# A new static order for an attention and two-MLP kernel: PSUM banks taken in turns, two-bank QK products, and small steps moved between engines

## The chip, the cores and the metric

The kernel runs as one program on one core of a Trainium2 chip. The metric is the device time of one execution in microseconds (us). Engines are named as the profile names them: PE (matrix multiply; PEld is its weight load), DVE (vector), ACT (scalar), POOL (GpSimd), and SP, whose queue issues nearly all DMAs. PSUM is the memory into which PE writes; the kernel holds it as one tile `pb` of eight banks of 512 words.

## The reference

```python
scores = scale * np.matmul(q, k.transpose(0, 1, 3, 2))        # 2 batches, 8 heads, 768 tokens, 64 dims
scores = np.where(keep, scores + bias, -1e9)                  # own 96 tokens back, and the first 8
a = np.exp(scores - max); a = a / (np.sum(a) + 1e-09)
x = np.matmul(a, v)                                           # laid out as (1536 tokens, 512)
h = x @ w_in                                                  # 512 -> 2048
P = a[0] + a[1]*h + a[2]*h**2 + a[3]*h**3
Q = 1.0 + np.abs(b[0])*np.abs(h) + np.abs(b[1])*h**2
x = (P / (Q + 1e-06)) @ w_out                                 # 2048 -> 512
h = x @ w_in2                                                 # 512 -> 1024
solu = h * softmax(h); ln = (solu - mean) / np.sqrt(var + 1e-06) * g_ln
out = ln @ w_out2                                             # 1024 -> 512
```

The weights come as 64-bit floats and are narrowed to 32 bits on the chip.

## The kernel before, in words

`record` writes down every piece of work as an operation (`op`) with an engine, an assumed duration, what it reads and writes, and a priority. `Plan.run` then goes through them as a list scheduler: at each step it takes the engine that can start earliest and, among the operations ready there within 0.15 us, the one with the smallest `due - lead`. The order in which it emits them is the static order of every engine, and the semaphores are put in for that order. Where two engines use the same PSUM bank, the emitted order also sets who goes first: the second one waits for the first, whether or not there is a data dependence. The planner before does not know of this; it lets two engines read a bank at the same time.

The work has these parts:

- Attention, in 48 units of one 128-token tile and two heads. `u_load` brings q, k (`qkt`) and v; `qk` (line 405) multiplies, DVE takes the bias and the minimum of both heads (`smax`, line 411), ACT exponentiates (418), DVE makes reciprocals (423, 424), POOL multiplies with them (`norm`, 429), PE transposes (446), ACT copies out (458), PE multiplies with v (`pv`, 453), and ACT and DVE split the result into a high and a low part (460 and line 82). q of each head is padded with zeros to 128 rows, so that one product per head runs over all 128 rows; both heads share one bank. The four units of a batch's first tile have 128 keys (n = 1), the others 256 (n = 2). The bias tables are made on DVE (369).
- The first MLP, over four blocks of 384 tokens: 64 steps of one block and one 128-wide slice f of the hidden dimension. Segments are (block 0, f 0 to 7), blocks 1, 2, 3 in full, and (block 0, f 8 to 15). A step has 12 products for h (574, 576, 580), the rational function on ACT and DVE (600 to 617; lines 602, 604, 607 read the bank of h on DVE and 600, 603, 606 on ACT), a low part on POOL (line 82, `g`), and three steps later 9 products into y (665, 666, 671). Attention of block 1 runs beside segment 0, of block 2 beside segment 1, of block 3 beside segment 2 (`UW`).
- 48 weight pieces of 128 x 512 (32 of the first MLP, 16 of the second), each loaded (485), scaled into a PSUM bank by ACT (509), its sign bits cleared in place by POOL (526), joined by two DVE operations (530, 518), cast to the high part by ACT (548) and subtracted to the low part by POOL (line 82, `w`).
- The second MLP, for twelve tiles: transposes of y (731), 24 products (750 to 752), softmax and normalisation on DVE and ACT (772 to 799), eight transposes (812), 24 products (834 to 836), copy and store (843, 845).

SP, like every engine, goes through its own list in the order emitted.

Of the kernel before, what the change touches and what calls it, by code (L numbers as in the profile page):

```python
# [30 lines left out]
UW = {1: (0, 7), 2: (8, 15), 3: (24, 15)}  # L31
# [3 lines left out]
M2 = (41, 22)  # L35

ZS = range(48)
# [3 lines left out]
WLEAD = 2.0  # L41


SLOW = (5.0, 1.2)
# [82 lines left out]
class Plan:  # L127
# [4 lines left out]
    SEM = 0.05  # L132
# [7 lines left out]
    def op(self, eng, lat, fn, r=(), w=(), new=(), occ=None, lock=False, lead=0.0, move=0.0, after=(), tag=""):  # L140
        o = Op()
        o.i, o.eng, o.lat, o.fn, o.lock, o.lead, o.move, o.tag = len(self.ops), eng, lat, fn, lock, lead, move, tag
# [44 lines left out]

    def settle(self, n):
# [13 lines left out]
    def run(self, emit=True):  # L202
        self.deadlines()
        self.pools = {p: [(0.0, s) for s in sl] for p, sl in self.slots.items()}
        for v in {v for o in self.ops for v in o.vals}:
            v.left, v.free = len(v.users), 0.0
# [6 lines left out]
        at = {e: 0.0 for e in ready}  # L213
# [3 lines left out]
        def add(o):  # L217
            o.t0 = max((d.end for d in o.deps), default=0.0) + self.SEM
            ready[o.eng].append(o)
# [5 lines left out]
        while left:  # L225
            best = None
            for e, l in ready.items():
                c = []
                for o in l:
                    t = max(o.t0, at[e])  # L230
                    ok = True
                    need = {}
                    for v in o.new:
# [3 lines left out]
                        need[v.pool] = need.get(v.pool, 0) + 1  # L237
                        fr = self.pools[v.pool]
                        if self.line[v.line][x][0] is not v or len(fr) < need[v.pool]:
                            ok = False  # L240
                            break
                        t = max(t, sorted(fr)[need[v.pool] - 1][0])
# [22 lines left out]
            at[e] = t + o.occ  # L265
            o.end = t + o.lat
            if o.lock:
                port = t + o.occ
            if e == "SP":
                dma = max(dma, at[e]) + o.move  # L270
                o.end = dma + o.lat
            for v in o.vals:
                v.left -= 1
# [26 lines left out]
def record(tc, es, const, qkv, w_in, w_out, w2_in, w2_out, coef, g_sb, nv, ident, out):  # L300
# [52 lines left out]
    def bias_keep():  # L353
# [11 lines left out]
        dve.tensor_scalar(out=kp, in0=kp, scalar1=-1.0, scalar2=-MASK, op0=ALU.add, op1=ALU.mult)  # L365
# [7 lines left out]
    op("DVE", 2.0, bias_keep, w=vt0)  # L373
    for p in range(4):
        op("DVE", 0.9, lambda p=p: bias_pair(p), r=vt0, w=[vbias[p]], lock=True)
# [4 lines left out]
    xs = {}  # L380
# [9 lines left out]
    def u_load(u):  # L390
        u.qk, u.v = Val("qk"), Val("v")
        w = 256 + u.w
        uop("SP", 2.0, lambda: sync.dma_start(out=qkt[u.qk.slot][:, 0:w], in_=qkv[u.t, u.p, :, 0:w]), occ=0.4,
# [796 lines left out]
```

## Time and profile before

| | us |
|---|---|
| median of 3 runs (568.31 to 568.39) | 568.36 |
| the profiled execution | 569.23 |
| its span, first to last instruction | 567.4 |
| busy: PE, DVE, ACT, POOL | 529.6, 429.2, 390.2, 223.9 |
| mean granted clock of PE, share of full speed | 0.989 |

The profiled execution lies 1.83 us above its own span and 0.87 us above the median. Matmuls overlap in the profile, so a busy PE is not PE at its peak. The span falls into six stages by what PE does: up to the first h product at 45.3 us (attention of block 0), segment 0 (to 97.6), segment 1 (to 192.2), segment 2 (to 287.4), segments 3 and 4 with their y products (to 417.4), and the second MLP, whose last 24 first products end at 538.1.

### The profile page before, as it was taken

How to read it: one execution, taken by the hardware profiler on the slowest of the kernel's cores; microseconds unless marked ns; L12 is line 12 of the kernel's file. 1: busy time of each engine (PE TensorE's matmuls, PEld its weight loads, DVE VectorE, ACT ScalarE, POOL GpSimd, SP SyncE). 2: the span in 40 equal slices, each digit the busy share in tenths (PEclk: the TensorE clock that was granted, in tenths of full speed). 3: DMA queues.
4: the chain of work that ended last, by engine and by line, in shares of the span. 5: the costliest groups of instructions: out<-in, count | busy, mean ns of one | idle time of the engine just before them, and what ended most of it. 6: DMA issues, size and time to landing. Idle time of an engine off the chain costs nothing.

```text
span 567.4 us, 8749 instructions
## 1 busy us (share of the span) xinstructions
PE 529.6 (93%) x2808; PEld 437.8 (77%) x2808; DVE 429.2 (76%) x1045; ACT 390.2 (69%) x903; POOL 223.9 (39%) x278
## 2 busy tenths in 40 slices
PE   4899998999989899999999989998999999999985
PEld 2567887878877688888887877877878888888865
DVE  6777888998999997677679999889866555555540
ACT  4788888898988888777788887877634444433331
POOL 3675456546677743332335563756400000000000
PEclk9999999999999999999999999999999999999989
DMA  7779255533444443110043230233001111000001
GB/s 247 244 259 324 89 167 161 165 102 94 130 160 152 134 133 114 36 58 26 2 149 130 75 115 34 76 111 104 25 21 39 40 54 37 22 35 20 18 20 43
DMA packets 28278, 56.24 MB, mean 99 GB/s; under 512 B 3520, under 2 KB 11968, under 8 KB 28224
## 3 DMA queue, kind: packets, MB, share of 16 engines
q1 hardware_dynamic: 28080, 55.59, 30.0%
q8 instruction: 24, 0.39, 0.3%
q14 instruction: 30, 0.25, 0.1%
q10 hardware_dynamic: 144, 0.00, 0.0%
HBM read 47.72 MB, written 7.86 MB: 98 GB/s over the span
## 4 chain that ended last, share of the span: by engine, by line
PE 51%; DVE 27%; ACT 15%; issue 4%; POOL 1%; DMA 1%; ACTq 0%; SPq 0%; POOLq 0%; DVEq 0%
PE pb L834 4%; PE pb L836 4%; PE pb L835 4%; PE pb L405 4%; PE pb L750 4%; PE pb L752 4%; PE pb L751 4%; DVE t L615 3%; DVE t L604 3%; DVE t L602 3%; PE pb L453 3%; PE pb L574 3%; PE pb L665 3%; PE pb L580 3%; DVE t L613 3%
## 5 line engine op out<-in xcount | busy, mean ns | idle before, releaser
L82 POOL TENSOR_TENSOR g<-t,g 128x384 fp32r<-128x384 f32 x64 | 69.4, 1084 | 79.9 <-ACT g L617 74.2
L574 PE MATMUL pb<-x,w 128*128 128x384 f32 x256 | 90.0, 352 | 5.4 <-DVE t L607 5.2
L576 PE MATMUL pb<-x,w 128*128 128x384 f32 x256 | 86.2, 337 | 0.0
L665 PE MATMUL pb<-w,g 128*128 128x512 f32 x192 | 78.3, 408 | 7.4 <-ACT g L617 6.3
L429 POOL TENSOR_SCALAR e<-e,st 128x256 f32<-128x256 f32 (+1 forms) x96 | 47.3, 505 | 75.0 <-DVE st L424 56.1
L666 PE MATMUL pb<-w,g 128*128 128x512 f32 x192 | 76.2, 397 | 0.0
L82 POOL TENSOR_TENSOR w<-wst,w 128x512 fp32r<-128x512 f32 x48 | 64.7, 1354 | 18.8 <-ACT w L548 16.2
L574 PEld LDWEIGHTS pb<-x,w 128*128 128x128 f32 x256 | 48.2, 188 | 14.0 <-DVE t L607 10.7
L580 PE MATMUL pb<-x,w 128*128 128x384 f32 x256 | 57.5, 346 | 0.0
L671 PE MATMUL pb<-w,g 128*128 128x512 f32 x192 | 57.2, 406 | 0.0
L405 PE MATMUL pb<-qk 128*128 128x256 f32 (+1 forms) x192 | 50.0, 392 | 6.7 <-DMA qk<-in_qkv 5.4
L602 DVE TENSOR_TENSOR t<-t,pb 128x384 f32<-128x384 f32 x64 | 35.1, 548 | 22.3 <-ACT t L603 20.8
L418 ACT ACTIVATE e<-e,st 128x256 f32<-128x256 f32 (+1 forms) x96 | 46.3, 486 | 5.3 <-DVE st L411 5.1
L665 PEld LDWEIGHTS pb<-w,g 128*128 128x128 f32 x192 | 36.3, 189 | 17.4 <-ACT g L617 9.3
L580 PEld LDWEIGHTS pb<-x,w 128*128 128x128 f32 x256 | 44.7, 188 | 6.2 <-issue 2.4
L576 PEld LDWEIGHTS pb<-x,w 128*128 128x128 f32 x256 | 48.3, 189 | 1.3
L405 PEld LDWEIGHTS pb<-qk 128*128 128x128 f32 x192 | 35.4, 208 | 12.9 <-DMA qk<-in_qkv 5.4
L606 ACT ACTIVATE pb<-pb 128x384 f32<-128x384 f32 x64 | 30.4, 476 | 20.9 <-DVE t L604 20.6
L600 ACT ACTIVATE t<-pb,coef 128x384 f32<-128x384 f32 x64 | 42.6, 666 | 2.6 <-PE pb L580 1.6
L617 ACT CAST g<-t 128x384 fp32r<-128x384 f32 x64 | 32.7, 512 | 16.9 <-DVE t L615 10.6
L607 DVE SCALAR_TENSOR_TENSOR t<-pb,coef,t 128x384 f32<-128x384 f32 x64 | 39.2, 612 | 6.8 <-ACT pb L606 6.1
L615 DVE SCALAR_TENSOR_TENSOR t<-t,coef,t 128x384 f32<-128x384 f32 x64 | 42.7, 667 | 0.7
(106 smaller groups left out, 1261.6 us busy)
## 6 DMA issues: line engine op xcount, KB each, us to landing
wst<-in_w_in SPq DMA_DIRECT2D x24, 512.0 KB, 4.3
wst<-in_w_out SPq DMA_DIRECT2D x24, 512.0 KB, 4.1
qk<-in_qkv SPq DMA_DIRECT2D x40, 256.0 KB, 3.2
v<-in_qkv SPq DMA_DIRECT2D x40, 128.0 KB, 2.5
y_d<-y SPq DMA_DIRECT2D x12, 256.0 KB, 2.7
y<-y_d SPq DMA_DIRECT2D x12, 256.0 KB, 2.6
out<-wst SPq DMA_DIRECT2D x11, 256.0 KB, 2.0
qk<-in_qkv SPq DMA_DIRECT2D x8, 192.0 KB, 3.3
```

What stands on the lines that cost most here:

```text
L82: eng.tensor_tensor(out=out, in0=a, in1=hi.bitcast(F32), op=ALU.subtract)
L405: pe.matmul(out=pb[:, u.s.slot, h * 256:h * 256 + w], lhsT=a[:, h * 128:(h + 1) * 128], rhs=a[:, 256:256 + w], start=True, stop=True)
L418: act.activation(out=e[:, h, 0:w], in_=e[:, h, 0:w], func=AF.Exp, scale=-1.0, bias=st[:, h:h + 1], accum_out=st[:, 2 + 2 * h:3 + 2 * h])
L429: pool.tensor_scalar(out=e[:, h, 0:w], in0=e[:, h, 0:w], scalar1=st[:, 6 + h:7 + h], scalar2=0.0, op0=ALU.mult, op1=ALU.add)
L574: pe.matmul(out=pb[:, g.h.slot, 0:n], lhsT=wt[wh.slot][:, cs[p]], rhs=xt[x[p][0].slot][:, 0:n], start=(p == 0), stop=False)
L576: pe.matmul(out=pb[:, g.h.slot, 0:n], lhsT=wt[wl.slot][:, cs[p]], rhs=xt[x[p][0].slot][:, 0:n], start=False, stop=False)
L580: pe.matmul(out=pb[:, g.h.slot, 0:n], lhsT=wt[wh.slot][:, cs[p]], rhs=xt[x[p][1].slot][:, 0:n], start=False, stop=(p == 3))
L602: op("DVE", 0.14 + 0.41 * k, lambda: dve.tensor_tensor(out=T(g.c), in0=T(g.c), in1=h(), op=ALU.mult), r=[g.h], w=[g.c], tag="ch")
L615: op("DVE", 0.15 + 0.41 * k, lambda: stt_(out=T(g.c), in0=T(g.c), scalar=coef[:, 0:1], in1=T(g.b), op0=ALU.add, op1=ALU.mult), r=[g.b], w= ...
L665: pe.matmul(out=pb[:, y[i].slot, :], lhsT=gt[g.gh.slot][:, c], rhs=wt[wh.slot], start=g.first, stop=False)
L666: pe.matmul(out=pb[:, y[i].slot, :], lhsT=gt[g.gh.slot][:, c], rhs=wt[wl.slot], start=False, stop=False)
L671: pe.matmul(out=pb[:, y[i].slot, :], lhsT=gt[g.gl.slot][:, c], rhs=wt[wh.slot], start=False, stop=g.last)
```

## The change

`Plan.run` keeps, for each value in a PSUM bank, the operation that used it last; a user on another engine may only start after that one's end. It also lets an operation that needs two buffers of one pool claim them against later-due ones, starts each engine's clock at a value of its own, and has other assumed durations, other gaps between the operations of POOL and DVE that it marks `lock` (these exclude each other in the plan), and a table of priorities (`LEADS`). In `record`: the attention units of blocks 0 and 3 take a bank for each head, and multiply 64 rows instead of 128; the bias tables go from DVE to ACT; `norm` goes from POOL to DVE for 19 of 48 units (`NDVE`); the sign bits of 22 of 48 weight pieces are handled by a second DVE operation instead of POOL's (`ZS`); 6 of 48 low parts go from POOL to DVE (`WDVE`); weight loads wait for the h products of the step before, and the second 16 weight pieces are spread over steps 8 to 22 (`WS`); the pieces of the second MLP are recorded over 17 steps instead of 22 (`M2`); and the weight pieces of segment 0 beyond the first four are recorded inside the steps.

```diff
+WS = (8, 14)
-UW = {1: (0, 7), 2: (8, 15), 3: (24, 15)}
+UW = {1: (0, 7), 2: (8, 15), 3: (25, 14)}
-M2 = (41, 22)
+M2 = (41, 17)
-ZS = range(48)
+ZS = (2, 4, 6, 8, 10, 12, 15, 17, 18, 20, 22, 24, 26, 28, 30, 32, 33, 34, 35, 36, 38, 40, 42, 44, 46, 47)
+START = ('hh',)
+BACK = (('y1', 'p'), ('y0', 'y2'))
+TWO = (3,)
+NDVE, WDVE = (3, 4, 5, 6, 7, 8, 9, 10, 11, 14, 15, 36, 38, 39, 40, 41, 42, 44, 46), (11, 20, 31, 42, 44, 45)
+BEGIN = {"PE": 2.0, "ACT": 5.0, "DVE": 3.4, "POOL": 1.0, "SP": 1.6, "X": 0.0}
+BANKS = ("h", "s", "p", "y0", "y1", "y2")
...
+                    for v in o.vals:
+                        if v.pool in BANKS and v.last is not None and v.last.eng != e:
+                            t = max(t, v.last.end + self.SEM)
...
-                        if o.lock:
-                            t = max(t, port)
-                        c.append((t, o))
+                        c.append((max(t, port - self.PORT) if o.lock else t, o, need))
+            for e, c in can.items():
+                c = [(t, o) for t, o, need in c if all(o.due - o.lead <= claims.get(p, 1e9) + CLAIM for p in need)]
...
+        dve.tensor_tensor(out=dz, in0=dz, in1=kp, op=ALU.add)
...
-            dve.scalar_tensor_tensor(out=bt[h], in0=dz, scalar=-8.0 * SLOPE[h], in1=kp, op0=ALU.mult, op1=ALU.add)
+            act.mul(bt[h], dz, -8.0 * SLOPE[h])
...
-                pe.matmul(out=pb[:, u.s.slot, h * 256:h * 256 + w], lhsT=a[:, h * 128:(h + 1) * 128],
-                          rhs=a[:, 256:256 + w], start=True, stop=True)
+                r = slice(h * 64, (h + 1) * 64) if two else slice(0, 128)
+                pe.matmul(out=score(h), lhsT=a[r, h * 128:(h + 1) * 128], rhs=a[r, 256:256 + w], start=True, stop=True)
...
-                pool.tensor_scalar(out=e[:, h, 0:w], in0=e[:, h, 0:w], scalar1=st[:, 6 + h:7 + h],
-                                   scalar2=0.0, op0=ALU.mult, op1=ALU.add)
+                (dve if ndve else pool).tensor_scalar(out=e[:, h, 0:w], in0=e[:, h, 0:w], scalar1=st[:, 6 + h:7 + h],
+                                                      scalar2=0.0, op0=ALU.mult, op1=ALU.add)
...
+        if nlo[0] - 1 in WDVE:
+            op("DVE", 0.68, lambda: minus(nc, dve, wt[lo.slot], src(), wt[hi.slot]), r=[st, hi], w=[lo], lock=True, lead=WLEAD, tag="wlo")
...
-            w_make(wseq[made[0]])
+            w_make(wseq[made[0]], [gs[-1].op] if gs else [])
...
-            make_to(2 * s + 4)
+            make_to(min(2 * s + 4, max(2 * SEGS[0][2], 2 * SEGS[0][2] + (s - WS[0]) * (32 - 2 * SEGS[0][2]) // WS[1])))
```

Three places of the order itself. POOL in block 0, before: its products with the reciprocals (line 429), sign bits of weight pieces (526) and low parts (82) alternate.

```order
L82 TENSOR_TENSOR w_95<-wst_157,w_94 128x512
L429 TENSOR_SCALAR e_214<-e_214,st_219 128x128 x2
L526 TENSOR_SCALAR wst_159<-wst_159 128x512
L82 TENSOR_TENSOR w_97<-wst_158,w_96 128x512
L429 TENSOR_SCALAR e_211<-e_211,st_220 128x256 x2
L429 TENSOR_SCALAR e_212<-e_212,st_221 128x256 x2
L526 TENSOR_SCALAR wst_156<-wst_156 128x512
L429 TENSOR_SCALAR e_213<-e_213,st_216 128x256 x2
```

The same place now (469 is the product with the reciprocals, 569 the sign bits, 97 the low part); from the fourth unit on, DVE does the products of block 0.

```order
L97 TENSOR_TENSOR w_93<-wst_156,w_92 128x512
L569 TENSOR_SCALAR wst_158<-wst_158 128x512
L97 TENSOR_TENSOR w_95<-wst_157,w_94 128x512
L97 TENSOR_TENSOR w_97<-wst_158,w_96 128x512
L97 TENSOR_TENSOR w_99<-wst_159,w_98 128x512
L469 TENSOR_SCALAR e_211<-e_211,st_216 128x256 x2
L469 TENSOR_SCALAR e_212<-e_212,st_217 128x256 x2
```

All but three units of block 0 left POOL, and the last two rows are already units of block 1. On DVE the same stretch now has, after the reciprocals (463, 464), the products (469), and for a piece without POOL's step two operations on the bank (556, 557) before the join (561).

```order
L556 SCALAR_TENSOR_TENSOR pb<-pb,wst_157 128x512
L557 SCALAR_TENSOR_TENSOR pb<-wst_157,pb 128x512
L451 ISA e_214,st_219<-pb,bt_202 128x128
L451 ISA st_219 128x1
L451 ISA e_214,st_219<-pb,bt_203 128x128
L451 ISA st_219 128x1
L561 SCALAR_TENSOR_TENSOR wst_157<-wst_157,pb 128x512
L463 TENSOR_SCALAR st_219<-st_219 128x2
L464 RECIPROCAL st_219<-st_219 128x2
L469 TENSOR_SCALAR e_214<-e_214,st_219 128x128 x2
```

Before, the piece had one operation on the bank (530) and no product stood there. The third place is PE's end. Before, after the output products of the tenth tile, the eight transposes of the eleventh tile (`wst_158`) are followed by four of the twelfth (`wst_156`), and only then come the products of the eleventh.

```order
L834 MATMUL pb<-w_123,lh_2892 128x512
L835 MATMUL pb<-w_122,lh_2892 128x512
L836 MATMUL pb<-w_123,ll_2894 128x512
L812 MATMUL pb<-ident,wst_158 128x128 x8
L812 MATMUL pb<-ident,wst_156 128x128 x4
L834 MATMUL pb<-w_109,lh_2891 128x512
L835 MATMUL pb<-w_111,lh_2891 128x512
```

Now the eleventh tile is `wst_156` and the twelfth `wst_158`; the last four transposes of the eleventh are followed at once by its products.

```order
L881 MATMUL pb<-w_123,lh_2892 128x512
L882 MATMUL pb<-w_122,lh_2892 128x512
L883 MATMUL pb<-w_123,ll_2894 128x512
L859 MATMUL pb<-ident,wst_156 128x128 x4
L881 MATMUL pb<-w_109,lh_2893 128x512
L882 MATMUL pb<-w_111,lh_2893 128x512
```

The twelfth tile's eight transposes moved behind those 24 products.

## Rows read from the trace of the kernel before

**Rows 1.** Windows, one stage each: stretch, length, busy us (instructions), PEclk, DMA.
```profile
0.00:45.30 45.30, 32.91 (x185) 22.46 (x185) 33.05 (x143) 31.32 (x98) 27.09 (x52) 0.96 0.75 246
45.30:97.60 52.30, 50.56 (x328) 41.58 (x326) 43.87 (x127) 45.91 (x122) 29.63 (x41) 1.00 0.56 184
97.60:192.20 94.60, 89.34 (x490) 73.83 (x488) 88.72 (x204) 82.64 (x196) 59.83 (x70) 0.98 0.43 138
192.20:287.40 95.20, 94.58 (x534) 79.58 (x535) 73.37 (x193) 74.88 (x180) 36.58 (x46) 1.00 0.20 62
287.40:417.40 130.00, 121.14 (x582) 103.09 (x582) 115.22 (x202) 100.78 (x200) 70.80 (x70) 1.00 0.26 89
417.40:538.10 120.70, 120.59 (x587) 100.04 (x586) 67.53 (x163) 48.02 (x99) 0.00 (x0) 1.00 0.10 33
538.10:567.40 29.30, 20.49 (x113) 17.27 (x111) 7.47 (x17) 6.61 (x14) 0.00 (x0) 0.90 0.09 30
```

**Rows 2.** Timeline of PE: start us, us, operation, count, [idle before <-releaser].
```profile
61.66 0.66 PE L453 MATMUL pb<-pt,v 128*64 128x128 f32 x8
62.25 0.96 PE L671 MATMUL pb<-w,g 128*128 128x512 f32 x3
63.05 1.03 PE L405 MATMUL pb<-qk 128*128 128x256 f32 x4
63.92 0.60 PE L446 MATMUL pb<-ident,e 128*128 128x128 f32 x4
...
293.03 0.86 PE L671 MATMUL pb<-w,g 128*128 128x512 f32 x3
293.73 0.87 PE L580 MATMUL pb<-x,w 128*128 128x384 f32 x4
...
297.22 0.86 PE L671 MATMUL pb<-w,g 128*128 128x512 f32 x3
```

**Rows 3.** Waits: engine line waited for: us in total, times, longest.
```profile
DVE t L602 <- ACT t L603: 20.8, 20, 2.5
```

**Rows 4.** Timeline of all engines around 337 us.
```profile
335.26 2.83 POOL L82 TENSOR_TENSOR w<-wst,w 128x512 fp32r<-128x512 f32 x2
336.88 1.64 DVE L611 SCALAR_TENSOR_TENSOR t<-t,t 128x384 f32<-128x384 f32 x1
339.64 0.50 PE L665 MATMUL pb<-w,g 128*128 128x512 f32 x1 [1.47 <-ACT g L617]
```

**Rows 5.** Groups by line and form: count, busy us, mean ns, idle before.
```profile
L530 DVE SCALAR_TENSOR_TENSOR pb<-pb,wst 128x512 int32<-128x512 int32 x48 | 33.2, 691 | 3.5 <-POOL wst L526 3.5
L82 POOL TENSOR_TENSOR w<-wst,w 128x512 fp32r<-128x512 f32 x48 | 64.7, 1354 | 18.8 <-ACT w L548 16.2 <-PE pb L671 1.3 <-PE pb L446 0.3
L526 POOL TENSOR_SCALAR wst<-wst 128x512 f32<-128x512 f32 x48 | 34.3, 715 | 12.1 <-ACT pb L509 7.2 <-PE pb L580 1.6
L429 POOL TENSOR_SCALAR e<-e,st 128x256 f32<-128x256 f32 x80 | 40.6, 520 | 64.4 <-DVE st L424 53.9 <-ACT t L610 3.9 <-PE pb L446 2.2
L369 DVE SCALAR_TENSOR_TENSOR bt<-t,t 128x264 bf16<-128x264 f32 x8 | 3.1, 422 | 0.0
L365 DVE TENSOR_SCALAR t<-t 128x264 f32<-128x264 f32 x1 | 0.3, 298 | 0.0
L423 DVE TENSOR_SCALAR st<-st 128x2 f32<-128x2 f32 x48 | 15.8, 329 | 1.5 <-ACT e L418 1.5
```

**Rows 6.** Single lines: durations in ns, least, median and most.
```profile
L611 DVE SCALAR_TENSOR_TENSOR t<-t,t x64: 535/551/1651, 57.3 to 405.8; 128x384 f32<-128x384 f32 x64
L423 DVE TENSOR_SCALAR st<-st x48: 151/164/981, 9.2 to 281.3; 128x2 f32<-128x2 f32 x48
```

**Rows 7.** Timeline of PE at the end.
```profile
543.44 1.04 PE L812 MATMUL pb<-ident,wst 128*128 128x128 f32 x8
547.22 0.66 PE L812 MATMUL pb<-ident,wst 128*128 128x128 f32 x4 [2.74 <-DVE wst L794]
554.82 0.60 PE L812 MATMUL pb<-ident,wst 128*128 128x128 f32 x4
```

More of the change, by code (lines that the diff above doesn't have):

```diff
@@ L141, in op @@
         o = Op()
-        o.i, o.eng, o.lat, o.fn, o.lock, o.lead, o.move, o.tag = len(self.ops), eng, lat, fn, lock, lead, move, tag
+        o.i, o.eng, o.lat, o.fn, o.lock, o.lead, o.move, o.tag = len(self.ops), eng, lat, fn, lock, lead + LEADS.get(tag, 0.0), move, tag
         o.occ = occ if occ is not None else lat - 0.1 if eng in ("ACT", "DVE") else lat
@@ L186, in deadlines, with late @@
             o.due = t
+    def late(self, d, o):
+        return self.SEM + (0.05 if o.eng == "POOL" else 0.0) + (0.1 if d.eng == "POOL" and o.eng == "PE" else 0.0)
     def settle(self, n):
@@ L217, in add @@
         def add(o):
-            o.t0 = max((d.end for d in o.deps), default=0.0) + self.SEM
+            o.t0 = max((d.end + self.late(d, o) for d in o.deps), default=0.0)
             ready[o.eng].append(o)
@@ L264, in run @@
             o.start = t
-            at[e] = t + o.occ
-            o.end = t + o.lat
+            wait = max(0.0, port - t - self.PORT) if o.lock else 0.0
+            at[e] = t + o.occ + wait
+            o.end = t + o.lat + wait
             if o.lock:
-                port = t + o.occ
+                port = o.end - (self.PORT2 if e == "POOL" else self.PORT)
             if e == "SP":
@@ L271, in run @@
                 o.end = dma + o.lat
+            o.prev = [v.last for v in o.vals if v.pool in BANKS and v.last is not None]
             for v in o.vals:
+                v.last = o
                 v.left -= 1
@@ L364, in bias_keep @@
         dve.tensor_tensor(out=kp[:, 0:8], in0=kp[:, 0:8], in1=gx, op=ALU.add)
-        dve.tensor_scalar(out=kp, in0=kp, scalar1=-1.0, scalar2=-MASK, op0=ALU.add, op1=ALU.mult)
+        dve.tensor_scalar(out=kp, in0=kp, scalar1=-1.0, scalar2=MASK * 256, op0=ALU.add, op1=ALU.mult)
+        dve.tensor_tensor(out=dz, in0=dz, in1=kp, op=ALU.add)
     def bias_pair(p):
         for h in (2 * p, 2 * p + 1):
-            dve.scalar_tensor_tensor(out=bt[h], in0=dz, scalar=-8.0 * SLOPE[h], in1=kp, op0=ALU.mult, op1=ALU.add)
+            act.mul(bt[h], dz, -8.0 * SLOPE[h])
     op("POOL", 0.9, bias_iota, new=vt0)
     op("DVE", 0.5, bias_rel, w=vt0)
-    op("DVE", 2.0, bias_keep, w=vt0)
+    op("DVE", 2.9, bias_keep, w=vt0)
     for p in range(4):
-        op("DVE", 0.9, lambda p=p: bias_pair(p), r=vt0, w=[vbias[p]], lock=True)
+        op("ACT", 0.75, lambda p=p: bias_pair(p), r=vt0, w=[vbias[p]], tag="bias")
     class U:
@@ L484, in w_load @@
         n = 1024 if wide else 512
-        op("SP", 2.0, lambda: sync.dma_start(out=wst[st.slot][:, 0:n], in_=src.bitcast(I32)), occ=0.4, new=[st],
-           move=2.0, tag="wld")
+        op("SP", 2.0, lambda: sync.dma_start(out=wst[st.slot][:, 0:n], in_=src.bitcast(I32)), occ=0.42, new=[st],
+           move=2.0, after=after, tag="wld")
         return st
-    nconv = [0]
+    nconv, nlo = [0], [0]
     def w_conv(st, new=()):
@@ L533, in w_conv @@
         if zero:
[L534 removed]
+            op("POOL", 0.7, signs, w=[st], lock=True, lead=WLEAD, occ=0.73, tag="wzs")
             op("DVE", 0.69, shift, r=[st], w=[bank], lead=WLEAD, tag="wbits")
```

112 lines of the change are left out of this document (64 added, 48 removed).

## The prediction

> **What bounds the kernel now.** I read the windows by stage first [rows 1], then the waits [rows 3], then the timeline at a few gaps [rows 2, 4, 7], and last the groups by line [rows 5, 6] for prices. In the windows the reader is to see four different limits.
>
> In the first stage nothing is full: PE 32.9, DVE 33.1, ACT 31.3 of 45.3 us. In segment 0 PE is at 50.6 of 52.3, DVE at 43.9. In segment 1 DVE is at 88.7 of 94.6, in segments 3 and 4 at 115.2 of 130.0: DVE is nearly the limit there. In segment 2 and in the second MLP PE is full (94.6 of 95.2, 120.6 of 120.7). The last 29.3 us have a hole.
>
> Busy PE hides slack, so I also need its real work. A step of the first MLP without attention takes 4.19 us from one group of line 671 to the next (293.03 to 297.22 [rows 2]), half of it h, half y. Segments 3 and 4 have 24 h groups and 28 y groups, 52 x 2.10 = 109 us, and before 417.4 some 36 products and 20 transposes of the second MLP, about 10 us at 0.23 us a product (line 671: 0.70 for three). So PE needs 119 of 130.0 us there: 11 us of slack, the largest of the middle.
>
> Why it stands idle there is in the timeline at 337 us [rows 4]. POOL ran two low parts (line 82) from 335.26 to 338.09. DVE's line 611 began at 336.88 and took 1.64 us where its median is 0.55 [rows 6]: it ended only after POOL did. What hung on it came late, and PE's next y product stood 1.47 us. The second cause is in the waits: line 602 on DVE waited 20.8 us in 20 places for line 603 on ACT [rows 3]. They share no data but the bank, so this is the turn at the bank that the old plan does not know.
>
> **The change part by part.** *Work that moves.* Onto DVE: 19 `norm` units, 18 with two heads of 256 columns and one of 128. The nearest row is 0.298 us for 264 columns (line 365) [rows 5]; 18 x 0.6 + 0.35 = 11.1. Then 22 second operations on a weight piece at line 530's 0.691: 15.2; six low parts, nearest the same row: 4.1; one more operation on the bias: 0.4. Off DVE: eight bias operations at 0.422: 3.4. Net +27 us on 429. Off POOL: 18 units x 2 x 0.520, one x 0.86, 22 x 0.715 and 6 x 1.354, together 43 of its 224 us. ACT gets eight bias tables, some 0.4 each by line 369's row, bounds 0.3 (line 365) and 0.7 (line 530), and loses none.
>
> DVE gets something back. Line 423 should take 0.164 us and takes 0.329 on average, 7.9 us over 48 [rows 5, 6]; lines 611, 613 and 615, 64 of each, meet the same [rows 4], and I put the time that DVE stands behind POOL at some 23 us in all, an estimate with 5 us for each of the three. A fifth of POOL's work leaves, so some 5 us of this go. The new `norm` on DVE can stand behind POOL as line 423 does: 38 instructions x 0.165 = 6 us more at worst.
>
> The Trainium skill ("SBUF — State Buffer", section "Who interferes with whom") says that DVE and GpSimd share one pair of ports as an exclusive lock, held for a whole instruction, and lists `tensor_scalar` among the operations that can take it. That speaks against this part, since the moved `norm` is a `tensor_scalar`; the trace agrees as far as line 423, also a `tensor_scalar`, which has been stretched to 0.981. By it the 6 us are to be counted, without it none; I count half.
>
> *Start (45.3 us).* The order puts 4 weight pieces instead of 9 before the first h product, which takes five scalings and four casts off ACT (some 0.6 each, between lines 365 and 530 in size, an estimate: -5.6), five pairs off DVE (-6.9) and most of POOL's work. Against it: ACT +3.2 for bias, DVE +5.3 for eleven `norm` units, +2.1 for three second operations, -3.4 for bias. One unit more is begun. The first minimum comes about 0.4 us later, behind DVE's extra operation and ACT's bias. ACT, which fills nearly all of 8 to 45 us, ends with 2 to 3 us less. Two banks a unit means that PE's next product waits for both minima of the unit before; PE has the transposes and `pv` of other units to do meanwhile. I take -3, from -6 to +1.
>
> *Segment 0 (52.3).* The five pieces come here: 12 instead of 7. DVE gets 5 x 2 x 0.691 + 6 x 0.691 and one low part more, and two units less, some 1.2 each (an estimate: two minima and two short steps): 43.9 + 9.3 = 53.2. It becomes the limit, where PE was. The loads of these pieces now stand on SP behind the stores of x and wait for the step before; v and q loads of block 1 queue behind them. The DMA engines have room (0.56 busy). I take +2, from 0 to +5.
>
> *Segment 1 (94.6).* Sixteen pieces as before (one fewer), spread evenly, eight with a second operation: DVE 88.7 + 5.5 + 0.7 - 1.4 = 93.5, less 2 to 3 us of standing behind POOL. That is all of the time there is. I take -0.5, from -3 to +6.
>
> *Segment 2 (95.2).* No pieces here any more. The two-bank products of block 3's twelve units save PE time. A full product takes 0.87 us for both heads (63.05 to 63.92). The nearest row for two parts of the array at once is `pv`, whose two heads use 64 columns each: eight instructions take 0.59 us (61.66 to 62.25), where eight of half the columns of the product's four would be 0.87 one after another. By that row a product takes 0.60 and saves 0.27; if both heads ran fully beside each other it would be 0.44; with no overlap 0.87 and nothing saved. Around `pv` the neighbours also stretch: line 671's three took 0.80 instead of 0.70 behind it [rows 2], and as much ahead; with that the product is at 0.80 and saves 0.07. So 12 units give 0.8 to 3.2, at most 5. DVE has room for the eight `norm` units (73.4 + 5). I take -3 with the better order, from -5 to 0. In block 0 PE is not the limit.
>
> The Trainium skill ("TensorEngine Tiling (Array Packing)", section "Key Properties") says that changing the tiling mode drains the engine. The 0.10 us behind `pv` agrees, and by that rule each of the new products pays it twice, so this term would be -0.8 rather than up to -3.2.
>
> *Segments 3 and 4 (130.0).* DVE 115.2 + 5 x 0.691 + 3 x 0.691 = 120.7, less some 3 us behind POOL: 118. PE needs 119. Both fit in 120; the stage takes 130 because they wait for each other [rows 3, 4]. An order that knows the turns should bring 124: -6, from -10 to +4.
>
> *The end.* PE stood 2.74 us at 547.22 for the normalisation of the last tile, with the eleventh tile's products queued behind [rows 7]. Now these come first, and the last tile's transposes after them. The chain from the last first product (538.1) to the normalised tile takes 9.1 us; two groups of 24 products (5.5 each) and transposes cover it. What comes late is then the copy of the twelfth tile's transposes, some 0.7 us (one pass over 512 columns, line 530's size). The 24 products between the rows at 547.22 and 554.82 took 7.2 us (7.6 less the four transposes) instead of 24 x 0.23 = 5.5, with a granted clock of 0.90 in this stage [rows 1]; behind the gap, half speed. If that goes with the gap, 1.7 more. I take -3.5, from -2 to -4.4.
>
> Sum: -3 + 2 - 0.5 - 3 - 6 - 3.5 = -14.0. 569.2 - 14.0 = 555.2 for a profiled execution, 0.9 less for the median: 554.5.
>
> **The rivals.** *DVE's added work decides (slower).* If DVE can't be filled better than before, segment 1 takes 93.5 / 0.938 = 99.7 (+5.1), segments 3 and 4 120.7 / 0.886 = 136.2 (+6.2), segment 0 53.2 / 0.94 = 56.6 (+4.3). With 0 at the start, -1 in segment 2 and -3.5 at the end that is +11: 579. It decides from the point where the stages' DVE share stays at 0.94 and 0.89. For it: the rows of segment 1. Against: the idle time of DVE there is the waits at banks, which the new order is about.
>
> *Only the end and segment 2 move.* The middle gives back on DVE what the turns bring: -3.5 - 2.5 = -6, 562.4. For it: turns are waited out already, and DVE does other work meanwhile.
>
> *All slack goes.* Each stage at its fullest engine: start -6, segment 0 +1, segment 1 -3, segment 2 -5, segments 3 and 4 -10, end -4.4: -27, 541. Against it: every stage chains three engines.
>
> *It does not do what it says.* The bank waits stand in the program in either case; if the new turns only swap who waits, and the end too waits elsewhere, 568.
>
> **How the numbers follow.** Forecast (548 to 560 by itself) 0.48; only end and segment 2 0.26; all slack 0.11; DVE decides 0.11, a part of which ends near zero; no effect 0.04. A measurement of this kernel tells 0.2%, 1.1 us, from no change. Faster: 0.48 + 0.26 + 0.11 = 0.85; same 0.04 with some of the DVE case, 0.05; slower 0.10. The range 545 to 566 holds the forecast, the small gain and the lower part of the full one; it leaves out most of DVE's case.
>
> **What would show it.** First h product at 41 to 44 us; segment 0 no shorter, with DVE over 0.93 busy; in segments 3 and 4 PE's waits for lines 617 and 607 down and the stage at 122 to 127; line 602's (now 649) wait for ACT well under 20.8; no gap before the last transposes, and the last 24 products of full width in 5.5 us; two-bank products at 0.55 to 0.80 us a unit. It is wrong if DVE's busy time grows by much more than 22 us, or if segments 1, 3 and 4 get longer while DVE is full.

## The result and the profile after

| | before | changed |
|---|---|---|
| median, us | 568.38 (4 runs, 568.31 to 568.51) | 560.81 (4 runs, 560.58 to 561.80) |
| the profiled execution, its span, us | 569.23, 567.4 | 560.58, 558.7 |
| busy: PE, DVE, ACT, POOL, us | 529.6, 429.2, 390.2, 223.9 | 525.9, 446.2, 392.8, 182.6 |

The ratio is 0.987 (0.9853 to 0.9887): 7.6 us faster, where 14.0 were forecast. The direction and the range held; the size is about half.

The windows of the changed kernel, cut at the same events as [rows 1] (columns as there):

```profile
0.00:46.10 46.10, 33.18 (x188) 20.25 (x189) 34.71 (x154) 30.28 (x102) 11.01 (x25) 1.00 0.59 190
46.10:99.70 53.60, 50.53 (x316) 39.45 (x314) 49.15 (x135) 49.16 (x123) 27.67 (x36) 1.00 0.64 206
99.70:193.70 94.00, 89.81 (x498) 73.64 (x496) 91.48 (x221) 83.22 (x201) 53.81 (x63) 1.00 0.49 153
193.70:286.80 93.10, 92.95 (x535) 74.57 (x536) 79.51 (x208) 74.42 (x179) 26.15 (x30) 1.00 0.20 60
286.80:409.90 123.10, 119.12 (x579) 103.31 (x577) 114.43 (x206) 99.66 (x197) 61.93 (x59) 1.00 0.29 94
409.90:527.20 117.30, 115.64 (x567) 96.16 (x566) 69.25 (x168) 48.34 (x98) 1.98 (x2) 1.00 0.10 32
527.20:558.70 31.50, 24.68 (x138) 20.77 (x136) 7.64 (x18) 7.70 (x16) 0.00 (x0) 0.97 0.10 36
```

Against [rows 1] the six terms of the forecast's sum read so:

| stage | forecast | measured |
|---|---|---|
| start | -3 | +0.8 |
| segment 0 | +2 | +1.3 |
| segment 1 | -0.5 | -0.6 |
| segment 2 | -3 | -2.1 |
| segments 3 and 4 | -6 | -6.9 |
| second MLP and end (last two rows) | -3.5 | -1.2 |

The measured column adds up to -8.7 us, the difference of the two profiled executions; the medians differ by 7.6 only, since the profiled execution of before is a long one. Of the 5.3 us that the column lacks of 14.0, 3.8 are the start and 2.3 the second MLP; segments 3 and 4 gave 0.9 more than forecast. PEclk is not to be read in the first row: the records of the granted clock begin later there. They say full speed (2.4 GHz) from 30.93 us on and one fall, at 556.6. In the kernel before they say full speed first from 19.05 us, with a fall to half from 25.88 to 29.29. How PE of the changed kernel went until then, in its timeline (columns as in [rows 2]):

```profile
8.28 1.11 PE L446 MATMUL pb<-qk 64*128 64x128 f32 x4 [2.03 <-DVE st L451]
18.72 1.43 PE L446 MATMUL pb<-qk 64*128 64x256 f32 x4 [1.50 <-DVE st L451]
26.50 1.56 PE L446 MATMUL pb<-qk 64*128 64x256 f32 x4 [0.96 <-DVE st L451]
31.70 0.70 PE L446 MATMUL pb<-qk 64*128 64x256 f32 x4
```

The same two products of a unit (four records in the trace) take 1.43 and 1.56 us before 30.93 and 0.70 behind it: that is the clock's half speed (1.2 GHz). And in front of them PE stands, each time for DVE's minimum (line 451) of the unit before, since a unit holds both banks.

The waits that answer to [rows 3], first of DVE, then of PE, and then three of PE in the kernel before:

```profile
DVE t L649 <- ACT t L650: 6.5, 8, 1.7
```
```profile
PE pb L446 <- DVE st L451: 5.6, 5, 2.0
PE pb L712 <- ACT g L664: 4.2, 7, 0.9
PE pb L621 <- DVE t L654: 1.7, 3, 0.8
```
```profile
PE pb L405 <- DVE st L411: 1.1, 2, 0.7
PE pb L665 <- ACT g L617: 6.3, 6, 2.2
PE pb L574 <- DVE t L607: 5.2, 8, 1.2
```

DVE's turn at the bank of h fell from 20.8 us to 6.5. PE's wait for the minima (first line) grew from 1.1 us to 5.6 with the two-bank products; its waits for g (second line) and for the bank of h (third) fell by 2.1 and 3.5.

The forms that answer to [rows 5] (columns as there), and the single lines that answer to [rows 6]:

```profile
L557 DVE SCALAR_TENSOR_TENSOR pb<-wst,pb 128x512 int32<-128x512 int32 x22 | 15.3, 696 | 0.8
L469 DVE TENSOR_SCALAR e<-e,st 128x256 f32<-128x256 f32 x36 | 12.1, 378 | 0.4
L469 DVE TENSOR_SCALAR e<-e,st 128x128 f32<-128x128 f32 x2 | 1.5, 812 | 0.0
L404 ACT ACTIVATE bt<-t 128x264 bf16<-128x264 f32 x8 | 2.8, 411 | 2.4 <-DVE t L400 2.4
```
```profile
L463 DVE TENSOR_SCALAR st<-st x48: 155/161/170, 9.7 to 279.2; 128x2 f32<-128x2 f32 x48
```

The added operations cost what the rows of before promised (0.696 against 0.691, 0.411 against some 0.4); `norm` on DVE is dearer (0.378 against 0.298), and two of its 38 operations took 1.34 and 1.38 us. The small operation that was stretched to 0.981 [rows 6] is now at 0.170 at most.

At the end the gap of [rows 7] is gone:

```profile
539.59 1.04 PE L859 MATMUL pb<-ident,wst 128*128 128x128 f32 x8
546.88 0.38 PE L881 MATMUL pb<-w,lh 128*128 128x256 f32 x1 [0.67 <-ACT wst L890]
```

The last tile's transposes wait for nothing, and the copy that the forecast saw come late costs 0.67 us where some 0.7 were expected. Behind the last first product PE has 31.96 us, and in them one group of 24 output products (5.5 at 0.23) and four transposes (0.5) more than before, where it had 29.44: 3.5 gained, the very term of the forecast. The stage gained only 1.2 because of its entry, for which the forecast had no term. Six transposes that PE did between and beside the last y products before now stand behind them: 0.65 us (from the last y product's end to the transposes of y it is 1.96 us, 0.76 of it a wait, where it was 0.55). With them come two waits; the kernel before has one of 0.46 there, ahead of its last y products:

```profile
411.03 1.09 PE L859 MATMUL pb<-ident,wst 128*128 128x128 f32 x8 [0.76 <-DVE wst L841]
```
```profile
434.83 0.66 PE L859 MATMUL pb<-ident,wst 128*128 128x128 f32 x4 [0.79 <-DVE ll L97]
```

-3.5 + 0.65 + 0.76 + 0.79 = -1.3, where -1.2 was measured. The transposes only crossed the line between two rows of the table, so segments 3 and 4 gained some 6 of their own.

### The profile page after: what moved, and what is told of

Same layout as the page of the kernel before. It is cut to its first block, busy times and chain, and to the rows that moved or that the text cites. A ratio compares the mean times of both kernels' runs of the same rounds, so it can differ in the third digit from the quotient of the medians.

```text
span 558.7 us, 8733 instructions
## 1 busy us (share of the span) xinstructions
PE 525.9 (94%) x2808; PEld 428.1 (77%) x2808; DVE 446.2 (80%) x1104; ACT 392.8 (70%) x911; POOL 182.6 (33%) x212
## 4 chain that ended last, share of the span: by engine, by line
PE 56%; DVE 28%; ACT 9%; issue 4%; POOL 1%; DMA 1%; SPq 0%; ACTq 0%; DVEq 0%; POOLq 0%
PE pb L881 4%; PE pb L621 4%; PE pb L883 4%; PE pb L882 4%; PE pb L627 4%; PE pb L797 4%; PE pb L799 4%; PE pb L798 4%; PE pb L718 4%; PE pb L623 4%; PE pb L712 4%; PE pb L713 3%; DVE wst L561 3%; PE pb L446 3%; DVE t L654 3%
## 5 line engine op out<-in xcount | busy, mean ns | idle before, releaser
L97 POOL TENSOR_TENSOR w<-wst,w 128x512 fp32r<-128x512 f32 x42 | 57.2, 1364 | 45.1 <-ACT w L591 44.0
L446 PE MATMUL pb<-qk 64*128 64x256 f32 (+3 forms) x192 | 46.2, 437 | 11.9 <-DVE st L451 5.6
L712 PEld LDWEIGHTS pb<-w,g 128*128 128x128 f32 x192 | 36.0, 188 | 14.3 <-ACT g L664 7.3
L647 ACT ACTIVATE t<-pb,coef 128x384 f32<-128x384 f32 x64 | 42.6, 666 | 6.2 <-PE pb L627 6.1
L469 POOL TENSOR_SCALAR e<-e,st 128x256 f32<-128x256 f32 (+1 forms) x58 | 28.0, 494 | 54.4 <-DVE st L464 39.9
L446 PEld LDWEIGHTS pb<-qk 64*128 64x128 f32 (+1 forms) x192 | 27.4, 210 | 23.0 <-DVE st L451 9.1
L656 ACT ACTIVATE t<-t,coef 128x384 f32<-128x384 f32 x64 | 39.5, 617 | 6.8 <-DVE t L654 6.6
L867 ACT CAST lh<-pb 128x512 fp32r<-128x512 f32 x24 | 13.8, 591 | 42.5 <-PE pb L859 42.5
```

Source lines behind the costliest of these rows:

```text
L97: eng.tensor_tensor(out=out, in0=a, in1=hi.bitcast(F32), op=ALU.subtract)
L446: pe.matmul(out=score(h), lhsT=a[r, h * 128:(h + 1) * 128], rhs=a[r, 256:256 + w], start=True, stop=True)
L647: op("ACT", 0.2 + 0.46 * k, lambda: act.activation(out=T(g.c), in_=h(), func=AF.Identity, scale=coef[:, 3:4], bias=coef[:, 2:3]), r=[g.h], ...
L656: op("ACT", 0.22 + 0.4 * k, lambda: act.activation(out=T(g.b), in_=T(g.a), func=AF.Ln, bias=coef[:, 6:7]), r=[g.a], w=[g.b], tag="ln")
L712: pe.matmul(out=pb[:, y[i].slot, :], lhsT=gt[g.gh.slot][:, c], rhs=wt[wh.slot], start=g.first, stop=False)
```

## The experiments

The stages of all profiled executions, cut at the start of the first h product of each segment and at the end of the last y product (0.4 us behind the cut above), and the ratio to the kernel before on the same chip:

| kernel | start | seg. 0 | seg. 1 | seg. 2 | 3 and 4 | rest | full clock from | ratio |
|---|---|---|---|---|---|---|---|---|
| before | 45.3 | 52.3 | 94.6 | 95.2 | 130.4 | 149.6 | 29.29 | 1 |
| changed | 46.1 | 53.6 | 94.0 | 93.1 | 123.5 | 148.4 | 30.93 | 0.9870 (0.9853 to 0.9887) |
| start, one bank | 42.6 | 64.3 | 93.3 | 92.2 | 126.5 | 148.5 | 19.72 | 0.9977 (0.9965 to 0.9989) |
| fill at the head | 46.5 | 53.9 | 93.1 | 93.1 | 123.5 | 148.6 | 31.86 | 0.9857 (0.9841 to 0.9872) |
| one bank, fill at the head | 42.0 | 62.8 | 92.7 | 92.2 | 126.4 | 148.4 | 19.68 | 0.9977 (0.9965 to 0.9989) |
| fill in the holes | 43.8 | 53.4 | 94.0 | 93.1 | 123.4 | 148.5 | 24.67 | 0.9791 (0.9778 to 0.9804) |
| start, one bank, later order kept | 42.6 | 53.5 | 93.1 | 93.1 | 123.5 | 148.5 | 18.65 | 0.9796 (0.9780 to 0.9811) |
| same with fill | 43.0 | 53.5 | 93.9 | 93.1 | 123.5 | 148.4 | 23.02 | 0.9812 (0.9790 to 0.9833) |
| block 3 one bank, order kept | 47.1 | 53.7 | 94.0 | 94.4 | 123.5 | 148.3 | 33.39 | 0.9889 (0.9871 to 0.9908) |
| no turns | 46.5 | 53.4 | 96.3 | 91.4 | 134.9 | 148.4 | 31.86 | 1.0104 (1.0072 to 1.0136) |
| moves undone | 42.3 | 59.1 | 93.0 | 93.6 | 127.1 | 147.1 | 20.74 | 0.9935 (0.9913 to 0.9957) |
| output lead 0 | 47.1 | 53.6 | 94.0 | 93.1 | 123.5 | 154.1 | 33.11 | 0.9956 (0.9939 to 0.9974) |
| signs on POOL, order kept | 47.1 | 57.5 | 99.0 | 93.7 | 128.7 | 148.4 | 31.74 | 1.0170 (1.0147 to 1.0194) |
| norm and low parts on POOL, order kept | 44.3 | 53.4 | 93.1 | 93.1 | 123.9 | 148.5 | 29.79 | 0.9840 (0.9818 to 0.9862) |

"Full clock from" is where the records last rise to full speed within the start.

Eight of these kernels run segment 1 alike, and it takes 93.1 us in three of them and 93.9 or 94.0 in five. The difference arises at one place, where a DVE and a POOL operation start within 20 ns of each other. DVE and then POOL in the changed kernel, and the same in the one with the fill at the head:

```profile
141.27 1.41 DVE L658 SCALAR_TENSOR_TENSOR t<-t,t 128x384 f32<-128x384 f32 x1
141.25 1.01 POOL L97 TENSOR_TENSOR g<-t,g 128x384 fp32r<-128x384 f32 x1
```
```profile
141.87 0.55 DVE L658 SCALAR_TENSOR_TENSOR t<-t,t 128x384 f32<-128x384 f32 x1
141.85 1.45 POOL L97 TENSOR_TENSOR g<-t,g 128x384 fp32r<-128x384 f32 x1
```

One of the two is stretched, and which one it is differs between runs of the same order. Where DVE's is the short one, all that follows comes some 0.8 us earlier; that much of a whole time is no effect of an edit here.

**The start: products in one bank again, or more work for PE.** My theory was that PE's clock held the start up, the rivals that the products' price, or other engines, did. Four kernels:

```diff
-START = ('hh',)
+START = ('h',)
```


> The changed kernel with one edit: block 0's scores are made in one bank a unit again, as before. Theory (clock): in the changed kernel the two-bank products of block 0 left holes in front of them and TensorE had its full clock only from 30.9 us, against 19.05 us in the kernel before; with the dense one-bank products the clock is back before 22 us and the first h product starts at 43.0 to 45.5 us (46.1 in the changed kernel, 45.3 before). First rival (the products' own price decides): a unit costs .87 again instead of .62, so the first h product starts at 47.5 us or later. Second rival (the loads, ScalarE or VectorE bound the start, whatever TensorE does): 46.1 +- 0.5.

The first h product came at 42.6, still earlier than the theory's 43.0, and the clock rose at 19.72; neither rival holds. But the edit takes away the wait for both banks together with the late clock, so it does not part the two. The whole stayed near the kernel before, since the planner had ordered everything behind it anew: segment 0 took 64.3 us. In it the clock fell to half three times, and one y group and one unit's scores more stood before the cut.

```diff
+    fill(10)    # ten products of ident by ident into a free bank, at PE's head
```


> The changed kernel with ten products of the identity by itself (128 columns, into a bank that nothing reads) on TensorE ahead of the first scores; added work, nothing left out. TensorE has nothing to do until 5.45 us, so they cost at most about 1 us. Theory (clock): the records show full speed before 15 us, and the first h product starts at 41 to 44.5 us (46.1), the whole at 556 to 559.5 us (560.8). Rival (loads, ScalarE or VectorE bound the start): the clock rises early all the same, but the first h product stays at 46.1 +- 0.7 and the whole at 560.8 +- 1.

A miss for the theory. The rival's times came (46.5, the whole 560.7), but not its condition: the clock was full from 4.55 to 7.96 only and then half until 31.86, with PE's waits standing as in the changed kernel. So this run does not decide between the two.

> Both edits: one bank a unit in block 0, and ten products of the identity ahead of the first scores. If the clock is what held the start, both kernels with the fill have the full clock early, and the difference of their first h products is the price of the two forms alone at full clock: 32 products of .87 against .62 where TensorE is the bound, up to 7 us at most, some 2 us as TensorE waits elsewhere for half of that time; so 43 to 46.5 us here. If loads, ScalarE or VectorE bound it: 46 +- 0.7, as in the other two.

42.0, below both ranges: full from 6.03 to 12.85, half to 19.68. The difference to the kernel with the head fill alone is 4.5 us, so it is no price of forms at equal clock; the clocks differ by 12 us. Against one bank without the fill it says more: up to the first h product all four engines run the same instructions in the same order, but for the ten products, and the clock rises for good at the same time (19.72 and 19.68). The full clock from 6.03 to 12.85 brought the first h product 0.53 us forward, and all of it is there at PE's 14.3 us already.

```diff
+            if k in (0, 1, 2, 4, 5, 6):
+                fill(3, [ulist[k].q])
```


> The changed kernel with the ten products at the head and three more behind each of the scores of units 0, 1, 2, 4, 5 and 6, all into a bank that nothing reads at that time. It is to tell whether the head alone keeps the clock up: if the head's effect is lost in the holes from 7 to 20 us, this kernel has its full clock earlier than the one with the head alone, and its first h product earlier by 0.5 us or more; if the head is enough, the 18 products (some 0.25 us each at full clock) are only in the way, and the first h product is later than with the head alone by 0 to 2 us.

43.8, 2.7 us earlier than with the head alone, as expected if the head's effect is lost in the holes: the clock was full from 7.60 to 14.43 and again from 24.67. The later stages are those of the changed kernel within 0.2 us. The two-bank products are still there, and so is the longest wait behind them (1.50 us); in the other holes the fillers stand. So about 2.3 us of the 46.1 go with the clock, 0.86 of them in front of the scores that start at 17.86 (18.72 in the changed kernel). A part may be the planner's, which ordered this start anew around the fillers.

**The same, with the later order kept.**

```diff
+ORDER = (0,7,14,21,8,15,1,22,2,34, ...    # one-bank order up to the first h product, then the changed kernel's
-        plan.run()
+        plan.follow(ORDER)
```


> Block 0's scores in one bank a unit, in the planner's order for that form up to the first h product; from there every engine's instructions in the order of the changed kernel, which is written out so that no planning intervenes. Where one bank in block 0 was planned anew, the first h product came at 42.6 us (46.1 in the changed kernel), yet the stretch from it to step 8 took 64.3 us instead of 53.6. Theory (that loss came from the other order behind the start and the clock's dips there, not from the start's form): first h product at 42 to 43.5 us, the stretch behind it 52.5 to 55.5, the whole 556.5 to 559.5 us (560.8). Rival (the early start only brings forward a wait for weights, which the stretch behind it pays back): first h product at 42 to 43.5 us, the stretch behind it 56.5 us or more, the whole 560 us or more.

The theory held: 42.6 and 53.5, and the later stages as in the changed kernel but for the 0.8 us of segment 1 told of above, which put the whole (556.1) just under the forecast range. It is one of the two fastest here. Its PE timeline against the one shown above:

```profile
16.17 2.77 PE L467 MATMUL pb<-qk 128*128 128x128 f32 x8
19.41 1.13 PE L467 MATMUL pb<-qk 128*128 128x256 f32 x4 [0.47 <-DVE st L472]
21.52 2.09 PE L467 MATMUL pb<-qk 128*128 128x256 f32 x8 [0.98 <-DVE st L472]
```

Two units' products stand back to back from 16.17 us, which two banks a unit forbid, and the full clock follows at 18.65.

**Does the clock set all of the start?**

```diff
+        if u.k < 4:
+            fill(2, [uops[-1]])          # behind the transposes; also behind the scores of units 1, 2, 4, 5
```


> The kernel with one bank a unit in block 0 and the later orders kept (556.1 us, first h product at 42.6, full clock from 18.65 us), with ten products of the identity at TensorE's head and two more in each of eight holes up to the sixth unit, into a bank that nothing reads at that time. Theory (the clock sets the start up to where it rises): full clock from before 10 us and kept, first h product at 40 to 41.8 us, the whole at 553.5 to 555.5 us. Rival (with the clock back at 18.65 the rest of the start is bound by ScalarE and VectorE): first h product at 42 to 43 us, the whole at 555.5 to 557 us.

The first h product came at 43.0, not before 42.6, which is the rival's time; the whole, 557.4, lies just over its range, with segment 1 at 93.9. But the clock was not kept: it was full from 5.95 to 19.6 us, half to 23.0. From the fourth to the ninth unit DVE's minima are 0.4 to 0.7 us ahead of the kernel without fill, and from the tenth on no longer. The planner also ordered this start anew. So the run does not show that the early clock is worth nothing; the pair with and without the fill at the head, above, prices it at 0.53 us for 6.82 us of full clock.

**Packed products in block 3.**

```diff
-        two, ndve = len(bank) == 2, u.k in NDVE
+        two, ndve = len(bank) == 2 and u.j == 0, u.k in NDVE
```


> The changed kernel with all orders kept as they are and one edit: in block 3 both heads' scores are multiplied as in the kernel before, two products over all 128 rows into one bank (the second bank stays claimed and empty). 16 units, 12 of them in segment 2, cost .87 instead of .62 each on TensorE. Theory (TensorE is the bound in segment 2, the packed form is worth its own time there): segment 2 at 95 to 96.5 us (93.1), the whole 3 to 4.5 us longer. Rival (these products stand in TensorE's holes, and segment 2 gained by its order): 93.1 +- 0.5, the whole within 1 us.

Between the two: segment 2 lost 1.3 us in 12 units, 0.11 a unit (block 3 has 12 units, not 16, and all of them stand in segment 2). (Of the 2.2 us by which the profiled span is longer, 1.0 is the start, told of below.) Two places of the changed kernel, then the same two with one bank:

```profile
222.39 0.60 PE L489 MATMUL pb<-ident,e 128*128 128x128 f32 x4
222.92 0.70 PE L446 MATMUL pb<-qk 64*128 64x256 f32 x4
223.55 0.44 PE L621 MATMUL pb<-x,w 128*128 128x384 f32 x1
223.83 0.34 PE L623 MATMUL pb<-x,w 128*128 128x384 f32 x1
...
228.28 0.94 PE L718 MATMUL pb<-w,g 128*128 128x512 f32 x3
229.14 0.70 PE L446 MATMUL pb<-qk 64*128 64x256 f32 x4
229.77 0.66 PE L496 MATMUL pb<-pt,v 128*64 128x128 f32 x8
230.36 0.44 PE L621 MATMUL pb<-x,w 128*128 128x384 f32 x1
```
```profile
223.64 0.60 PE L510 MATMUL pb<-ident,e 128*128 128x128 f32 x4
224.08 1.03 PE L467 MATMUL pb<-qk 128*128 128x256 f32 x4
224.76 0.52 PE L642 MATMUL pb<-x,w 128*128 128x384 f32 x1
225.12 0.34 PE L644 MATMUL pb<-x,w 128*128 128x384 f32 x1
...
229.57 0.93 PE L739 MATMUL pb<-w,g 128*128 128x512 f32 x3
230.34 1.02 PE L467 MATMUL pb<-qk 128*128 128x256 f32 x4
231.29 0.66 PE L517 MATMUL pb<-pt,v 128*64 128x128 f32 x8
231.88 0.44 PE L642 MATMUL pb<-x,w 128*128 128x384 f32 x1
```

Read from start to start. Between transposes and h the packed group (222.39 to 223.83) takes 1.44 us, the other (223.64 to 225.12) 1.48. Next to `pv` it is 2.08 (228.28 to 230.36) against 2.31. The packed product itself takes 0.63 each time, but what stands ahead of it is 0.09 longer (0.53 against 0.44, 0.86 against 0.77). Between full-width neighbours nearly all is given back; beside `pv`, which is packed too, 0.23 stays. Of the 12 units six give 0.03 to 0.04, four give 0.23, and the other two 0.28 and -0.18. The Trainium skill ("TensorEngine Tiling (Array Packing)", section "Key Properties") says that a change of tiling mode drains the engine; these rows agree. By that rule the prediction had this term at -0.8; -1.3 was measured.

**What carries the middle: the turns or the moves?**

```diff
-BANKS = ("h", "s", "p", "y0", "y1", "y2")
+BANKS = ()
```


> The changed kernel planned without the rule that engines use a bank only in turns (the planner's list of such banks is empty); the work and its engines stay as in the changed kernel. Theory (the rule and the order that comes of it carry segments 3 and 4): segments 3 and 4 up to the first product of the second network 110.5 to 114 us (107.6; before 113.6), the whole 564 to 568 us. Rival (the moves between engines carry it): 107.6 +- 1.5 there, the whole within 560.8 +- 2.5.

More than the theory: segments 3 and 4 took 134.9 us, 11.4 longer, and the whole (573.5) is slower than before the change. PE's waits:

```profile
PE pb L621 <- DVE t L654: 10.3, 11, 1.9
PE pb L712 <- ACT g L664: 5.3, 7, 2.2
```

It stands for the bank of h, for which it stood 1.7 us in the changed kernel. The leads and costs around the rule are those made for a plan with it, so this prices the rule within this planner, not against the old one.

```diff
-ZS = (2, 4, 6, ...)     START = ('hh',)    TWO = (3,)    NDVE, WDVE = (3, 4, ...), (11, ...)
+ZS = range(48)          START = ('h',)     TWO = ()      NDVE, WDVE = (), ()
-    op("ACT", 0.75, lambda p=p: bias_pair(p), ...
+    op("DVE", 0.9, lambda p=p: bias_pair(p), ...
```


> The changed kernel's planner (turns, costs, leads, pacing) with all moved work put back: one bank a unit in every block, biases, signs, normalizing and low halves on the engines they had before. Theory (the order carries most of the gain behind the start): VectorE's stalls behind GpSimd are back, but segments 3 and 4 stay at 107 to 110.5 us, the whole 559 to 564 us. Rival (the moves carry it): 111.5 us or more there, the whole 565 to 569 us, as before the change.

Between the two: 564.4, half of the gain. Of the 6.9 us of segments 3 and 4, 3.3 are there without any move; the other 3.6 need the moves or the order made for them. The start is at 42.3 with all work where it was: 3.0 under the kernel before by the order alone, though segment 0 behind it is 6.8 longer.

```diff
-op("DVE", 1.27, bits, r=[st], ...
+op("DVE", 1.27, lambda: (signs(), shift()), r=[st], ...    # signs() is POOL's
```


> All orders kept as in the changed kernel and one edit: the 22 conversions whose signs VectorE makes in two instructions of its own are given the older form, one instruction on GpSimd that VectorE then waits for, and one on VectorE. VectorE has 22 instructions of some .69 us less, GpSimd 22 of some .65 more. Theory (VectorE gained because it stands behind GpSimd less): segments 3 and 4 take 125 to 128 us (123.5 to the end of the last y product), the whole 2 to 6 us longer. Rival (where signs are made matters little, the order does it): 123.5 +- 0.7, the whole within 1 us.

The direction held, the size did not: 16.8 us. This line of DVE's waits is new:

```profile
DVE pb L594 <- POOL wst L590: 29.8, 22, 2.3
```

DVE waits 1.35 us at each of the 22 signs for POOL's queue. An order made with that in mind would hide part of it: planned anew, with all moves undone, the whole took 564.4. What the run says is that in this order DVE's second operation of 0.69 us is cheaper than the trip to POOL.

```diff
-(dve if ndve else pool).tensor_scalar(out=e ...
+pool.tensor_scalar(out=e ...                 # and minus(nc, pool, ...) for the low parts
```


> All orders kept as in the changed kernel and one edit: the 19 units' normalizing and the 6 low halves of weights that went to VectorE are issued on GpSimd again (11 of the units in block 0's start). Theory (these moves shorten a chain that TensorE waits for in the start, and cost VectorE little): first h product at 47 to 49 us (46.1 to 47.1), segments 3 and 4 124 to 126 us (123.5), the whole 1 to 5 us longer. Rival (VectorE is nearer its limit than GpSimd, so that the moves cost as much as they save): within 1 us of the changed kernel in every stage.

Theory and rival both fell. The start is 1.8 us shorter (44.3), the rest within 0.4 but for the 0.8 of segment 1 told of above, the whole 0.984. Timeline of the changed kernel, DVE and then POOL:

```profile
20.02 1.54 DVE L469 TENSOR_SCALAR e<-e,st 128x128 f32<-128x128 f32 x2
21.48 0.41 DVE L451 CUSTOM_DVE_ANT_0 e<-pb,bt 128x256 f32<-128x256 f32 x1
```
```profile
20.21 1.27 POOL L97 TENSOR_TENSOR w<-wst,w 128x512 fp32r<-128x512 f32 x1 [0.77 <-ACT w L591]
```

The two small `norm` operations on DVE are through only with POOL's low part, at about 21.5, and the next unit's minimum comes behind them. With `norm` on POOL that minimum starts at 20.05, 1.43 us earlier. The Trainium skill ("SBUF — State Buffer", section "Who interferes with whom") lets `tensor_scalar` stand behind a whole POOL instruction; this row agrees (1.34 us for the second of the two, 0.29 for the first). Two of the 38 `norm` operations were stretched, by some 1 us each, where the forecast had 3 us in all; it did not see that one of them would stand in the start's chain.

**The output products.**

```diff
-LEADS = {"o": -35.2, ...
+LEADS = {"o": 0.0, ...
```


> The changed kernel with one number of the planner edited: the lead of the second network's output products from -35.2 to 0, so that they stand one tile earlier again (three groups behind the last first product, not four). Nothing ahead of the second network's third tile moves. Theory (the later output products fill the wait for the last tile's normalizing): that wait of some 2.7 us in front of the last transposes is back, and the time from the last y product to the end is 150.5 to 152.5 us (148.4), the whole 2 to 4 us longer than the changed kernel. Rival (putting them off costs at the entry, where little is ready, what it saves at the end): 147 to 149.5 us, the whole within 1 us.

The theory's wait came back to the hundredth, and the price was higher: 5.7 us more from the last y product on, and 5.2 for the whole instead of 2 to 4.

```profile
545.05 1.10 PE L859 MATMUL pb<-ident,wst 128*128 128x128 f32 x4 [2.74 <-DVE wst L841]
```

The records show the clock at half from 545.11 to 548.52 behind it, as behind the gap of [rows 7]. With 29.63 us behind the last first product the end is 3.7 longer, as before the change. The other 2.0 lie ahead of it, where the rival hoped to gain: each tile's first products now follow closer on its transposes, PE's weight loads wait for the low part of y, and from the fourth tile on the 24 products take 6.0 us instead of 5.6:

```profile
PEld pb L799 <- DVE yl L97: 3.9, 9, 0.4
```

The changed kernel does not have this line. Of the entry's two waits the first (0.76) is 0.75 here and the second (0.79) is gone, so the second came with putting the output products off.

## Why the prediction was half right

- **Start: wrong.** The step that failed is "PE has the transposes and `pv` of other units to do meanwhile", and with it "In block 0 PE is not the limit". PE had too little of it in the first 30 us: in the start it stood 4.7 us in four places for the minima, and the clock stayed at half until 30.93. With one bank a unit and the same moves the four waits are 2.6 us, the clock is full from 18.65, and the start is 42.6; I gave the two-bank wait no price. That 42.6 is near the forecast's -3 is in part luck: up to there DVE works 33.54 us and ACT 30.48 (33.05 and 31.32 before), where 2.9 less and 2 to 3 less had been worked out (four pairs of weight steps left DVE and nine `norm` units came, not five and eleven), and without any move the start is 42.3. That the clock counts can also be read without any edit: the changed kernel and the one with one bank in block 3 run the same instructions up to the first h product. Their PE timelines agree within 0.1 us up to the scores at 29.03 and 28.94; in the second the clock rose 2.46 us later, and the first h product came 1.0 later.
- **Segment 0: the number near (+1.3 for +2), the reason not.** DVE was to become the limit with 53.2 us of work; it has 49.15 of 53.60, a share of 0.92, beside PE's 0.94 and ACT's 0.92. What sets this stage was not tested.
- **Segment 1: right** (-0.6 for -0.5), with DVE at 91.48 us where 90.5 to 91.5 had been worked out; it is -1.5 where the two operations of segment 1 shown above fall the other way.
- **Segment 2: near (-2.1 for -3), the packed part overrated.** I took the row of `pv`, 0.27 a unit; it was 0.11, near the lower bound of 0.07, since the switch is paid where the neighbours are full-width. The other 0.8 is not the packing's; whether it is the order's or the moves' was not parted.
- **Segments 3 and 4: right** (-6.9, of which some 0.65 is transposes that moved out). The step that DVE and PE wait for each other at banks held: without the rule of turns this stage is 11.4 longer. DVE did not decide: it could be filled to 0.93 (114.4 of 123.1 us) where it stood at 0.89. Its added work was 17 us net in all, where 27 less some 5 had been worked out.
- **End: right at its place (-3.5), the stage short.** The entry's 1.6 us of waits were in no term.

Of the rivals none is the result. "Only the end and segment 2 move" lies nearest in time (562.4), but by the wrong stages: segments 3 and 4 gave their 6.9. (The forecast's own sum gives 554.3 for the median, not 554.5; nothing hangs on it.)

Open is what segment 0 loses when the planner starts from another start (64.3, 62.8 and 59.1 against 53.6). In the first two one y group and one unit's scores more stand before the cut (some 3 us); in all three PE's waits there are longer (6.7, 8.2 and 8.8 us against 3.1). What the clock's falls add was not parted. One bank in block 0 together with `norm` on POOL and the later order kept was not run.

## What to carry over

When a buffer scheme makes an engine wait for its reader, ask first what other work that engine has at that very time; an average over the stage (PE 33 of 46 us) does not say it, and in a start PE's clock adds to the price. Where a planner makes the order, one edit moves everything behind it: keep the order written out when you want the price of the edit alone. And a product packed into half of the rows paid here mainly beside work that is packed alike.

## What was not expected of the hardware

- Products that nobody reads made the kernel faster: with 28 of them in the start, planned anew, the first h product came 2.3 us earlier, and the whole was 0.9791 against 0.9870.
- A later clock costs 0.41 us of the start for each us: 1.0 for 2.46, at the same instructions, and 0.95 for 2.18 with the output lead at 0. Early in the start it counts for less: full speed from 6.03 to 12.85 brought 0.53.
- Two products over 64 rows each into two banks start 7 ns apart in the trace (205.082 and 205.089 us) and a unit takes 0.63 us; the change of form costs the neighbour ahead 0.09.
- Two DVE operations on 128 columns took 1.54 us beside one POOL instruction of 1.27.
- Of a DVE and a POOL operation that start within 20 ns of each other now the one is stretched (0.55 to 1.41 us), now the other (1.01 to 1.45), and the kernel's time differs by 0.8 us with it.
